# Linear attention with a feed-forward network: the first two query chunks loaded and prepared ahead of the values

## The chip, the cores and the metric

The kernel runs on one core of a Trainium2 chip. The time is that of the device for one launch, in microseconds (us). Engines are named as the profile does: PE is TensorE (its weight loads, which overlap, are PEld), DVE is VectorE, ACT is ScalarE, POOL is GpSimd, SP is SyncE. Loads and stores are DMA transfers that one of the engines issues.

## The reference

Eight batches of cosformer attention (8 heads, 576 rows, 64 columns each) are followed by a multiplicative feed-forward network (FFN) over all 4608 rows:

```python
def phi(x, c, s):
    r = np.maximum(x, 0.0)
    return np.concatenate([r * c, r * s], axis=-1)
q_p = phi(q, cos_w, sin_w)          # cos and sin of pi/2 * row / 576
k_p = phi(k, cos_w, sin_w)
kv = np.einsum('bhsf,bhsd->bhfd', k_p, v)
z = np.sum(k_p, axis=2)
num = np.einsum('bhsf,bhfd->bhsd', q_p, kv)
den = np.einsum('bhsf,bhf->bhs', q_p, z)[..., None] + 1e-06
x = (num / den)                      # heads side by side: 4608 x 512
out = (((x @ w1) * (x @ w2)) @ w3) @ w_out
```

The features of a row are 128 wide: 64 cosine and 64 sine values. No row of a batch can be finished before all keys and values of its batch have gone into the sums kv and z.

## The kernel before

**The work and its stages.** Each batch is cut into chunks of 128 rows (the fifth has 64), with all heads side by side. The chunks of batch 0 go through these steps, each with a name and line that the profile shows:

- Features of a chunk (`features`): VectorE makes the cosine half (L273), ScalarE the sine half (L277). With `scalar_heads=4`, ScalarE makes the sine half of four heads and VectorE that of the other four (L280). `prep_k` and `prep_q` call it for keys (kp) and queries (qp).
- `prep_v` copies a chunk of the values next to a column of ones (va, L300), so that one matmul gives kv and z together.
- `kv_first` runs the 40 key-value matmuls of batch 0 (5 chunks x 8 heads, L325) into two PSUM banks, four heads in each, kva and one half of a pnum tile, and copies them to kvs (L331).
- `q_tr` transposes the features of a query chunk with eight matmuls into a PSUM tile pst (L339); the copy to qpT is left to the caller by VectorE (first returned function) or ScalarE (second, L342). `q_tr_halves` does the same in two halves with a VectorE copy each (L352, L353).
- `num` makes the numerator and denominator of a chunk with eight matmuls (L368), and VectorE divides (L384 to L386) into xblk. With `chain=False` the division is returned, to be placed later.
- `x_tr` transposes xblk with four matmuls (L420) and copies the result into xT (L422), by VectorE or by ScalarE. xT is what the FFN multiplies (`products`, L465).

**The order.** The kernel is scheduled by hand: each engine carries out its instructions in the order in which the program gives them. First comes the setup, with the loads of batch 0. SyncE issues the keys in f32; GpSimd issues the rest with a conversion to bf16: values, the last 64 rows of the values, query chunks 0 and 1, chunks 2 and 3, then the FFN weights. Further loads (`other_loads`) are let go by a GpSimd copy that reads the first xblk. `idle_mms(n)` runs n matmuls on zeros whose result nobody reads, to keep TensorE busy while it has nothing to do.

Then comes the part in which the change lies, written out by hand: features of the keys, values, sums, features and transposes of the first query chunks, the first two numerators. After it the FFN begins, in 40 + 24 x 8 groups; between groups stand the steps of attention that the planner put into numbered slots. Slot 1, after the first 16 FFN matmuls, holds `x_tr` of chunk 1, the transposes of query chunk 3 and `num` of chunk 2; slot 3 and slot 5 hold the next ones:

```python
at(1, lambda: x_tr(0, 1, by_vector=True), lambda: q_tr(0, 3, evac=False)[1](), lambda: num(0, 2))
at(3, lambda: x_tr(0, 2), lambda: num(0, 3))
at(5, lambda: x_tr(0, 3))
```

PSUM tiles: ps_tr holds two pst tiles, used in turn by all transposes; ps_att holds one pnum tile, ps_first the numerator of chunk 0.

Of the kernel before, what the change touches and what calls it, by code (L numbers as in the profile page):

```python
# [68 lines left out]
def kernel(  # L69
# [11 lines left out]
    nc = tc.nc  # L81
# [49 lines left out]
    def load_first(eng, t, src, c0=0, n=4, b=0):  # L131
        rows = src[b, :, 0:512, :].rearrange("h (p j) d -> p h j d", j=4)
        eng.dma_start(out=t[:, :, c0:c0 + n, :].rearrange("p h j d -> p h (j d)"),  # L133
                      in_=rows[:, :, c0:c0 + n, :].rearrange("p h j d -> p h (j d)"))

    def load_first4(eng, t, src, b=0):
        eng.dma_start(out=t[0:64, :, 4, :], in_=src[b, :, 512:S, :].rearrange("h p d -> p h d"))
# [19 lines left out]
    v0 = raw[0, "v"] = ld.tile([P, H, NCH, D], BF16, name="vs")  # L157
    load_first(nc.sync, k0, k)
    load_first4(nc.sync, k0, k)
    load_first(nc.gpsimd, v0, v)  # L160
    zeros = const.tile([P, 512], BF16, name="zeros")
    nc.vector.memset(zeros[:], 0.0)
    va_bufs, kp_bufs, qp_bufs = [], [], []
# [19 lines left out]
    def idle_mms(n):  # L183

        for _ in range(n):
            nc.tensor.matmul(unread[:, :], lhsT=zeros[:, 0:128], rhs=zeros[:], start=True, stop=True)

    idle_mms(27)
    cosv, sinv = _trig_tables(nc, const)
    identb = const.tile([P, P], BF16, name="identb")  # L190
    load_first4(nc.gpsimd, v0, v)
    load_first(nc.gpsimd, q0, q, 0, 2)
    make_identity(nc, identb[:])
    load_first(nc.gpsimd, q0, q, 2, 2)
    def load_w12(c0, n):
# [58 lines left out]
    feat = {}  # L254

    def feat_of(b):
        if b not in feat:
            feat[b] = (kp_bufs[b % 2], qp_bufs[b % 2], va_bufs[b % 2])
        return feat[b]
# [8 lines left out]
    def features(b, dst, src, c, cos=True, sin=True, scalar_heads=H):  # L268

        R = ROWS[c]  # L270
        at = c if b in (0, B - 1) else NCH + c
        if cos:
            nc.vector.tensor_scalar(out=dst[:R, c, :, 0:D], in0=src[:R, :, c, :], scalar1=0.0,  # L273
                                    scalar2=cosv[:R, at:at + 1], op0=ALU.max, op1=ALU.mult)
        if sin:
            n = scalar_heads
            nc.scalar.activation(out=dst[:R, c, 0:n, D:F], in_=src[:R, 0:n, c, :], func=ACTF.Relu,  # L277
                                 scale=sinv[:R, at:at + 1], bias=0.0)
            if n < H:
                nc.vector.tensor_scalar(out=dst[:R, c, n:H, D:F], in0=src[:R, n:H, c, :],  # L280
                                        scalar1=0.0, scalar2=sinv[:R, at:at + 1],
                                        op0=ALU.max, op1=ALU.mult)
# [6 lines left out]
    def prep_k(b, c):  # L289
        features(b, feat_of(b)[0], raw[b, "k"], c)  # L290

    def prep_q(b, c):
        features(b, feat_of(b)[1], raw[b, "q"], c)
        if c in dma_q(b):
            transpose_q(b, c)
# [21 lines left out]
    def kv_first():  # L317

        kp, qp, va = feat[0]
        kvs = sm.tile([P, H, D + 1], BF16, name="kvs", bufs=2)  # L320
        kvb = ps_att.tile([P, 2, 512], FP32, name="pnum")
        halves = (kva[:, :], kvb[:, 0, :])
        for c in range(NCH):
            for h in range(H):
                nc.tensor.matmul(halves[h // 4][:, ds((h % 4) * 65, 65)], lhsT=kp[:, c, h, :],  # L325
                                 rhs=va[:, c, h, 0:D + 1], start=(c == 0 and h % 4 == 0),
                                 stop=(c == NCH - 1 and h % 4 == 3))
        att_of(0)["kvs"] = kvs
        yield
        for half in range(2):  # L330
            nc.scalar.copy(out=kvs[:, 4 * half:4 * half + 4, :], in_=halves[half][:, 0:260])  # L331
        yield

    def q_tr(b, c, evac=True):
        R = ROWS[c]
        qp = feat[b][1]
        pst = ps_tr.tile([P, 8, 128], BF16, name="pst")
        for h in range(H):
            nc.tensor.transpose(pst[:, h, :], qp[:, c, h, :], identb[:])  # L339
        dst, src = att_of(b)["qpT"][:, :, ds(columns_of(b, c), R)], pst[:, :, 0:R]  # L340
        on_vector = lambda: nc.vector.tensor_copy(out=dst, in_=src)
        on_scalar = lambda: nc.scalar.copy(out=dst, in_=src)  # L342
        if evac:
            on_vector()
        return on_vector, on_scalar

    def q_tr_halves(b, c):

        for half in range(2):
            pst = ps_tr.tile([P, 8, 128], BF16, name="pst")  # L350
            for i in range(4):
                nc.tensor.transpose(pst[:, i, :], feat[b][1][:, c, 4 * half + i, :], identb[:])  # L352
            nc.vector.tensor_copy(out=att_of(b)["qpT"][:, ts(half, 4), ds(columns_of(b, c), 128)],  # L353
                                  in_=pst[:, 0:4, :])

    def num(b, c, chain=True, in_two=False):
        rows = out_rows(b, c)
        R = ROWS[c]
        at = columns_of(b, c) - rows.start
        qpT, kvs = att[b]["qpT"], att[b]["kvs"]  # L360
        if b == 0 and c == 0:
            nt = ps_first.tile([P, 2, 512], FP32, name="pfirst")
        else:
            pool = more_att[0] if more_att and order_of(b).index(c) % 2 == 0 else ps_att
            nt = None if in_two else pool.tile([P, 2, 512], FP32, name="pnum")
        banks = [ffn_tile(), ffn_tile()] if in_two else [nt[:, g, :] for g in range(2)]
        for h in range(H):
            nc.tensor.matmul(banks[h // 4][:, ds((h % 4) * 65, 65)], lhsT=qpT[:, h, ds(at, 128)],  # L368
                             rhs=kvs[:, h, :], start=True, stop=True)
        if b < 2:  # L370
            rows, R = slice(0, P), P
        if in_two:
            parts = [(slice(g, g + 1), t[rows, 0:260].rearrange("p (g h e) -> p g h e", g=1, e=65))
                     for g, t in enumerate(banks)]
        else:
            parts = [(slice(0, 2), nt[rows, :, 0:260].rearrange("p g (h e) -> p g h e", e=65))]
        xblk = sm.tile([P, 2, 4, D], BF16, name="xblk", bufs=4)
        att[b]["x"][c] = xblk

        def normalize():  # L380
            den = sm.tile([P, 2, 4], FP32, name="den")
            for g, n4 in parts:
                G = g.stop - g.start
                nc.vector.tensor_scalar_add(out=den[rows, g], in0=n4[:, :, :, 64], scalar1=1e-6)  # L384
                nc.vector.reciprocal(out=den[rows, g], in_=den[rows, g])
                nc.vector.tensor_tensor(out=xblk[rows, g], in0=n4[:, :, :, 0:D],  # L386
                                        in1=den[rows, g].unsqueeze(3).to_broadcast([R, G, 4, D]),
                                        op=ALU.mult)

        if chain:  # L390
            normalize()
        return normalize
# [11 lines left out]
    def x_tr(b, c, by_vector=False):  # L404
        R, rows = ROWS[c], out_rows(b, c)
        xblk = att[b]["x"].pop(c)
        xf = xblk[:].rearrange("p g h d -> p (g h d)")
        if b % 2 == 0:
            slot = S * b + 128 * c
        else:  # L410
            slot = S * b + (0 if c == 4 else 64 + 128 * c)
        t, o = divmod(slot, 512)
        if t not in xT:
            xT[t] = xtp.tile([P, 4, 512], BF16, name="xT")
        if b >= 2 or (b, c) in ((0, 4), (1, 3)):
            nc.sync.dma_start_transpose(out=xT[t][:, :, ds(o, R)], in_=xf[rows])
            return
        pst = ps_tr.tile([P, 8, 128], BF16, name="pst")
        for kc in range(4):
            nc.tensor.transpose(pst[:, kc, :], xf[:, ts(kc, 128)], identb[:])  # L420
        copy = nc.vector.tensor_copy if by_vector else nc.scalar.copy
        copy(out=xT[t][:, :, ds(o, R)], in_=pst[:, 0:4, rows])  # L422
# [168 lines left out]

    for c in range(NCH):
        prep_k(0, c)
    for c in range(NCH):
        prep_v(0, c)
    kv_steps = kv_first()
    next(kv_steps)
    q0f = feat[0][1]
    features(0, q0f, q0, 0, scalar_heads=4)
    next(kv_steps)  # L600
    prep_q(0, 1)
    idle_mms(2)
    q_tr_halves(0, 0)
    prep_q(0, 2)
    idle_mms(1)
    num(0, 0)
    q_tr(0, 1, evac=False)[1]()
    other_loads(att[0]["x"][0][:, 0, 0, 0:1])
    features(0, q0f, q0, 3, sin=False)
    features(0, q0f, q0, 3, cos=False)  # L610
    idle_mms(2)
    x_tr(0, 0, by_vector=True)
    num(0, 1)
    q_tr(0, 2, evac=False)[1]()
    ps_ffn = []
    for stack in first:
        stack.close()
# [82 lines left out]
```

## Time and profile before

| what | value |
|---|---|
| time, median of 3 | 247.64 us (247.55 to 247.78) |
| span of the profiled execution | 245.9 us |
| PE busy | 238.0 us, 97% |
| DVE busy | 138.2 us, 56% |
| ACT busy | 130.3 us, 53% |
| POOL busy | 94.1 us, 38% |
| granted TensorE clock | 1.0 |
| first FFN matmul | 16.0 us after the start of the span |

The shares are over the whole span. Nearly all of it is the FFN, in which TensorE goes without a pause; the change touches only the first 18 us. There the timeline, the chain of waits and the time from issue to landing of each load are the views to read. Times in them are counted from the start of the span. A transfer's landing is its issue plus its time to landing.

### The profile page before, as it was taken

Reading aid. Unit: us, or ns where it says so; the run is one execution under the profiler, and the core shown is the slowest. Engines: PE = TensorE matmul, PEld = TensorE weight load, DVE = VectorE, ACT = ScalarE, POOL = GpSimd, SP = SyncE. Lnnn points to the kernel's source line nnn. Section 1 sums busy time; section 2 is a strip of 40 time slices with the busy share of each in tenths; the row PEclk is TensorE's granted clock in tenths of the full one; section 3 lists DMA queues with packets and bytes.
Section 4 is the critical chain, followed back from the end, with each engine's and each line's share of the span. In section 5 each row is a group of like instructions: output and inputs, shape, how many; then the busy total and the mean of one; then the engine's idle time right before and its main releaser. Section 6 shows DMA issues by size and latency. Waiting matters only on the chain.

```text
span 245.9 us, 5011 instructions
## 1 busy us (share of the span) xinstructions
PE 238.0 (97%) x1842; PEld 130.7 (53%) x1872; DVE 138.2 (56%) x344; ACT 130.3 (53%) x266; POOL 94.1 (38%) x196
## 2 busy tenths in 40 slices
PE   8799999999999999999999999999999999999994
PEld 3479555566965445455554545455545554444443
DVE  7775663668976655656674565657564544312420
ACT  2675324856943693576377546663674233434332
POOL 7655352124412162228032603451331005978700
PEclk9999999999999999999999999999999999999999
DMA  6999999999989979979999999999996227998923
GB/s 194 182 197 200 206 206 202 194 185 170 151 156 119 187 106 170 182 107 161 182 130 136 178 136 133 168 129 187 143 122 119 54 54 224 256 300 277 290 87 128
DMA packets 86200, 41.22 MB, mean 168 GB/s; under 512 B 53792, under 2 KB 82720, under 8 KB 86176
## 3 DMA queue, kind: packets, MB, share of 16 engines
q0 software_dynamic: 37008, 27.20, 71.4%
q1 hardware_dynamic: 49168, 13.71, 35.9%
q8 instruction: 14, 0.23, 0.4%
q14 instruction: 10, 0.08, 0.1%
HBM read 38.80 MB, written 9.44 MB: 196 GB/s over the span
## 4 chain that ended last, share of the span: by engine, by line
PE 92%; DMA 3%; issue 1%; DVE 1%; POOL 1%; ACT 0%; POOLq 0%
PE ffnps L465 50%; PE ffnps L535 24%; PE ffnps L240 6%; PE pnum L368 4%; PE pnum L308 4%; DMA qs<-in_q_dram 3%; PE pst L226 1%; PE pst L339 1%; PE pst L420 1%; PE ffnps L551 1%; POOL vs L133 0%; DVE xblk L386 0%; PE pfirst L368 0%; PE ffnps L368 0%; DVE qpT L353 0%
## 5 line engine op out<-in xcount | busy, mean ns | idle before, releaser
L465 PE MATMUL ffnps<-xT,w2b 128*128 128x512 bf16 (+2 forms) x337 | 75.0, 343 | 0.5
L465 PE MATMUL ffnps<-xT,w1b 128*128 128x512 bf16 (+2 forms) x335 | 74.5, 343 | 0.3
L522 DVE TENSOR_TENSOR abT<-asb,ffnps 128x512 bf16<-128x512 bf16 x64 | 43.9, 685 | 49.1 <-PE ffnps L465 44.8
L518 ACT CAST asb<-ffnps 128x512 bf16<-128x512 f32 x64 | 37.4, 585 | 52.5 <-PE ffnps L465 45.1
L535 PE MATMUL ffnps<-w34b,abT 128*128 128x512 bf16 x270 | 63.5, 379 | 0.5
L570 POOL COPY seen<-mark 1x1 bf16<-1x1 bf16 x50 | 9.0, 179 | 101.1 <-ACT mark L568 101.1
L465 PEld LDWEIGHTS <-w2b 128*128 128x128 bf16 x344 | 30.9, 98 | 26.8
L465 PEld LDWEIGHTS <-w1b 128*128 128x128 bf16 x344 | 30.9, 98 | 26.6
L535 PEld LDWEIGHTS <-abT 128*128 128x128 bf16 x280 | 26.0, 98 | 27.9
L542 ACT COPY osb<-ffnps 128x512 f32<-128x512 f32 x35 | 20.4, 584 | 31.4 <-PE ffnps L535 31.4
L277 ACT ACTIVATE qp<-qs,sinv 128x512 bf16<-128x512 bf16 (+2 forms) x40 | 28.1, 716 | 1.6 <-DMA qs<-in_q_dram 1.6
L277 ACT ACTIVATE kp<-ks,sinv 128x512 bf16<-128x512 bf16 (+1 forms) x35 | 24.8, 719 | 4.1 <-DMA ks<-in_k_dram 4.1
L386 DVE TENSOR_TENSOR xblk<-pnum,den 128x512 bf16<-128x512 f32 (+1 forms) x37 | 25.6, 691 | 1.3
L450 POOL DMA_DIRECT2D out_dram<-osb x42 | 22.1, 531 | 3.0 <-issue 2.1
L300 POOL COPY va<-vs 128x512 bf16<-128x512 bf16 (+1 forms) x30 | 17.8, 629 | 6.4 <-DMA vs<-in_v_dram 4.3
L368 PEld LDWEIGHTS <-qpT 128*128 128x128 bf16 x320 | 15.4, 98 | 8.7 <-DVE qpT L353 0.6
L384 DVE TENSOR_SCALAR den<-pnum 128x8 f32<-128x8 f32 (+1 forms) x37 | 6.1, 164 | 22.2 <-PE pnum L368 21.9
L273 DVE TENSOR_SCALAR qp<-qs,cosv 128x512 bf16<-128x512 bf16 (+1 forms) x40 | 16.7, 425 | 0.7 <-DMA qs<-in_q_dram 0.7
L368 PE MATMUL pnum<-kvs,qpT 128*128 128x65 bf16 x296 | 15.7, 194 | 0.1
L240 PE MATMUL ffnps<-woutb,w3T 128*128 128x512 bf16 x61 | 15.1, 379 | 0.2
L273 DVE TENSOR_SCALAR kp<-ks,cosv 128x512 bf16<-128x512 bf16 (+1 forms) x35 | 12.3, 370 | 2.5 <-DMA ks<-in_k_dram 2.5
L308 PEld LDWEIGHTS <-kp 128*128 128x128 bf16 x280 | 11.3, 98 | 3.8
(88 smaller groups left out, 182.5 us busy)
## 6 DMA issues: line engine op xcount, KB each, us to landing
out_dram<-osb POOLq DMA_DIRECT2D x16, 256.0 KB, 4.3
out_dram<-osb POOLq DMA_DIRECT2D x24, 128.0 KB, 3.8
qs<-in_q_dram POOLq DMA_DIRECT2D x8, 256.0 KB, 6.6
ks<-in_k_dram POOLq DMA_DIRECT2D x6, 320.0 KB, 6.0
qs<-in_q_dram POOLq DMA_DIRECT2D x6, 320.0 KB, 7.6
vs<-in_v_dram POOLq DMA_DIRECT2D x6, 320.0 KB, 6.0
ks<-in_k_dram POOLq DMA_DIRECT2D x6, 256.0 KB, 7.9
vs<-in_v_dram POOLq DMA_DIRECT2D x6, 256.0 KB, 6.4
```

Source lines behind the costliest of these rows:

```text
L240: nc.tensor.matmul(acc[:, :], lhsT=w3T[:, lc % 4, :], rhs=woutb[:, lc, :], start=(lc == 0), stop=(lc == 7))
L273: nc.vector.tensor_scalar(out=dst[:R, c, :, 0:D], in0=src[:R, :, c, :], scalar1=0.0, scalar2=cosv[:R, at:at + 1], op0=ALU.max, op1=ALU.mult)
L277: nc.scalar.activation(out=dst[:R, c, 0:n, D:F], in_=src[:R, 0:n, c, :], func=ACTF.Relu, scale=sinv[:R, at:at + 1], bias=0.0)
L308: nc.tensor.matmul(kvt[:, h // 4, ds((h % 4) * 65, 65)], lhsT=kp[:, c, h, :], rhs=va[:, c, h, 0:D + 1], start=(i == 0 and h % 4 == 0), sto ...
L368: nc.tensor.matmul(banks[h // 4][:, ds((h % 4) * 65, 65)], lhsT=qpT[:, h, ds(at, 128)], rhs=kvs[:, h, :], start=True, stop=True)
L386: nc.vector.tensor_tensor(out=xblk[rows, g], in0=n4[:, :, :, 0:D], in1=den[rows, g].unsqueeze(3).to_broadcast([R, G, 4, D]), op=ALU.mult)
L450: eng.dma_start(out=rows[:, :, cols], in_=osb[64 * i:64 * i + rows.shape[0], :, cols])
L465: nc.tensor.matmul(out, lhsT=w[:, kc, ts(jc, 128)], rhs=x[:, kc, tok], start=(kc == 0), stop=(kc == 3))
L518: nc.scalar.copy(out=asb[:], in_=aT[:, :])
L522: nc.vector.tensor_mul(out=abT[:, jc, :], in0=asb[:], in1=bT[:, :])
L535: nc.tensor.matmul(ops[:, :], lhsT=abT[:, jc, ts(ms, 128)], rhs=w34b[:, jc, :], start=(jc == 0), stop=(jc == 7))
L542: nc.scalar.copy(out=osb[:, ms % 2, :], in_=ops[:, :])
```

## The change

The loads of query chunks 0 and 1 are issued before those of the values. Their features, and the transposes of both chunks, stand ahead of the value copies and the key-value matmuls, so that they can be made while the values land. The key-value sums are copied out of PSUM by ScalarE and VectorE, half each, instead of by ScalarE alone. The features of chunk 2 and 3, the copies of the transposes and the division of chunk 1 take other places in the queues; `x_tr` of chunk 0 is copied by ScalarE instead of VectorE, and the number of idle matmuls changes from 2, 1 and 2 to 7, 1 and 1.

```diff
-    load_first(nc.gpsimd, v0, v)
+    load_first(nc.gpsimd, q0, q, 0, 2)
...
+    load_first(nc.gpsimd, v0, v)
     load_first4(nc.gpsimd, v0, v)
-    load_first(nc.gpsimd, q0, q, 0, 2)
     make_identity(nc, identb[:])
     load_first(nc.gpsimd, q0, q, 2, 2)
...
-        for half in range(2):
-            nc.scalar.copy(out=kvs[:, 4 * half:4 * half + 4, :], in_=halves[half][:, 0:260])
+        for half, copy in enumerate((nc.scalar.copy, nc.vector.tensor_copy)):
+            copy(out=kvs[:, 4 * half:4 * half + 4, :], in_=halves[half][:, 0:260])
...
     for c in range(NCH):
         prep_k(0, c)
+    feat_of(0)
+    q0f = feat[0][1]
+    features(0, q0f, q0, 0, scalar_heads=4)
+    prep_q(0, 1)
+    idle_mms(7)
+    q_tr(0, 0, evac=False)[1]()
+    second = q_tr(0, 1, evac=False)[1]
     for c in range(NCH):
         prep_v(0, c)
     kv_steps = kv_first()
     next(kv_steps)
-    q0f = feat[0][1]
-    features(0, q0f, q0, 0, scalar_heads=4)
     next(kv_steps)
-    prep_q(0, 1)
-    idle_mms(2)
-    q_tr_halves(0, 0)
-    prep_q(0, 2)
+    second()
     idle_mms(1)
     num(0, 0)
-    q_tr(0, 1, evac=False)[1]()
+    prep_q(0, 2)
     other_loads(att[0]["x"][0][:, 0, 0, 0:1])
-    features(0, q0f, q0, 3, sin=False)
-    features(0, q0f, q0, 3, cos=False)
-    idle_mms(2)
-    x_tr(0, 0, by_vector=True)
-    num(0, 1)
+    idle_mms(1)
+    divide = num(0, 1, chain=False)
+    x_tr(0, 0)
+    divide()
     q_tr(0, 2, evac=False)[1]()
+    features(0, q0f, q0, 3)
```

## The prediction

> **What bounds the kernel now.** I read the page first: the shares by engine, then the chain that ended last. TensorE is busy for 97% of the span and carries the chain nearly alone:
>
> ```profile
> PE 92%; DMA 3%; issue 1%; DVE 1%; POOL 1%; ACT 0%; POOLq 0%
> ```
>
> The 3% of DMA is one wait of 8 us at the start. So I asked for the chain in order of time (start us, length us, what), where the change lies:
>
> ```profile
> 3.56 8.04 DMA qs<-in_q_dram
> ...
> 11.63 0.35 DVE qp L273
> ...
> 12.20 0.41 PE pst L352 x4
> ...
> 13.11 0.30 PE pfirst L368 x4
> ...
> 13.78 0.18 DVE den L384
> ...
> 14.22 0.70 DVE xblk L386
> ...
> 14.97 0.40 PE pst L420 x4
> 15.37 0.36 PE pnum L368 x8
> 15.73 0.45 PE pst L339 x8
> 16.18 0.89 PE ffnps L465 x16
> ```
>
> The reader is to see two things. The start is bound by the landing of the first two query chunks at 11.6 us; from there one chain runs through features, transposes, numerator, division and transpose to the first FFN matmul (its group starts at 16.01 us in the timeline). And from 16 us on the chain is TensorE alone. The waits of TensorE and of its weight loads, asked for from 16 us to the end, hold one row in all:
>
> ```profile
> PEld L339 <- ACT qp L277: 0.4, 1, 0.4
> ```
>
> So there is no slack later that could swallow a delay or lose a gain: the end moves by what TensorE's queue gains or loses before about 18 us. Next I read when the loads land, from the tiles' answers (values, then queries):
>
> ```profile
> DMA to landing us min/median/max: 7.5/8.0/8.4
> DMA to landing us min/median/max: 8.0/8.0/11.9
> ```
>
> Values of rows 0 to 511 are issued at 1.28 and land at 9.7; their last 64 rows, issued at 2.87, land at 10.4; query chunks 0 and 1, issued at 3.56, land at 11.6; chunks 2 and 3, issued at 5.03, at 13.0. Last the timeline (start, us, what), for durations and for the queue of ScalarE:
>
> ```profile
> 9.87 1.09 DVE L300 COPY va<-vs 128x512 bf16<-128x512 bf16 x5
> 12.05 0.35 ACT L331 CAST kvs<-kva 128x260 bf16<-128x260 f32 x1
> 12.57 1.34 ACT L277 ACTIVATE qp<-qs,sinv 128x512 bf16<-128x512 bf16 x2
> 14.23 1.01 ACT L342 COPY qpT<-pst 128x1024 bf16<-128x1024 bf16 x1 [0.32 <-PE pst L339]
> 17.27 0.61 PE L339 MATMUL pst<-identb,qp 128*128 128x128 bf16 x8
> ```
>
> The value copies begin when VectorE is done with the key features, just after the landing; a transposed chunk costs ScalarE 1.01, a sine half 0.72 (0.62 from start to start, two in 1.34); and the transpose of query chunk 3 starts at 17.27.
>
> [...] the first key-value copy, whose sums ended at about 11.7, waits behind a sine half and starts at 12.05. [...] here the values, issued at 1.28, land 2.9 us after the keys' 6.84. [...] In this trace 1.3 us idle before 10.20 cost no clock; the gaps that I find below are under 0.7 us, so I cost them no clock.
>
> **The change part by part.**
>
> *Loads reordered.* The same three transfers stand in the ring before 11.6, the pair of query chunks now first. The pair took 11.6-10.4 = 1.2 us behind the values, the last 64 rows 0.66. So the pair should land at 9.7-1.2 = 8.5, the values at 11.61-0.66 = 10.95 and their last rows at 11.6. The landing of query chunks 2 and 3 (13.0) and of the weights behind them doesn't move.
>
> *Features and transposes of chunks 0 and 1 moved ahead.* ScalarE is busy with the key sines till then: five from 6.91, a start each 0.61, free at 9.99. Its queue: half-width sine of chunk 0, 9.99 to 10.50; sine of chunk 1, 10.40 to 11.12. VectorE is free at 9.86; its cosines (0.35) and half sine (0.28) end by 10.7, before the values. TensorE: 27 idle matmuls to 8.9, seven more at 0.21 to 10.2, hidden in waiting. Transposes of chunk 0 at 10.55, of chunk 1 at 11.12+0.05 = 11.17, eight at 0.056, free at 11.61. ScalarE copies chunk 0 out from 11.20 to 12.21. This takes 1.5 us of work (11.61 to 13.11) off the query path, but it is queued ahead of the key-value matmuls.
>
> *Key-value sums.* First value copy 10.95 to 11.25, its matmuls could start at 11.3, but stand behind the second transpose: 11.61. They start 0.031 apart, 40 of them: the last at 12.86 (10.20 to 11.44 before). So the sums come 1.42 us later than before.
>
> *Copies on two engines.* ScalarE's half 12.97 to 13.33; VectorE's half (0.43, L314) 13.09 to 13.52. One engine would need 0.26 longer start to start, so this saves about 0.1. The numerator's first four heads go at 13.38, the last four at 13.57, last start 13.68, denominator 0.23 later at 13.91 (before 13.78: **+0.13**). Moving the query work ahead thus exchanges a chain that ends at 13.78 for one that ends at 13.91.
>
> *Division and its transpose.* Same operations: product at 14.35 to 15.04, transpose 15.09 (numerator 1 now stands before it, in a wait). The copy to xT goes from VectorE (0.42) to ScalarE (0.59): 15.51 to 16.10, FFN starts at **16.15** against 16.01. Transposes of chunk 2 need a cosine that stands behind the product on VectorE (14.95 to 15.30) and go at 15.35, free at 15.8: hidden.
>
> *Features of chunk 3 moved behind.* ScalarE's queue after its key-value half, in order: the copy of chunk 1, 13.23 to 14.24; sine 2, to 14.9; the xT copy, 15.51 to 16.10 as above; the copy of chunk 2, 16.00 to 17.01; sine 3, 16.92 to 17.63. In the kernel before, sine 3 ran at 15.14. The transposes of chunk 3 wait for it: **17.68** instead of 17.27. Ahead of them on TensorE are 16 FFN matmuls and four transposes, done at 17.3 (16.15+0.94+0.22). So TensorE stands about 0.37 us, and behind that wait in its queue are numerator 2 and all the FFN. From there, as before, 0.70 to the next FFN matmul: 18.39 instead of 17.98, **+0.41**.
>
> *Rest.* The later loads are let go by the first product, 0.13 later[...]. Fewer idle matmuls at 14 us and one division fewer in a slot change no sum. End: 247.64+0.41 = 248.05.
>
> **The rivals.**
>
> *Forecast: ScalarE's order costs what the earlier queries gain* (0.60). +0.41, with some 0.15 of handoffs to either side, so it lies just within 0.2% (0.50 us), or just over.
>
> *The values become the bound* (0.28). The margin is small: TensorE is free for the sums at 11.61, which a landing up to 11.28 meets, and I work out 10.95. [...] Landing between 11.6 and 12.1 delays all by 0.3 to 0.8: 248.4 to 248.9. For it: nothing in this trace shows the loads in this order. Against it: the sum of the three transfers is measured, and only the short last rows follow the values.
>
> *The hiding pays* (0.12). If the sums went with the landing of the values at 11.3 instead of behind the transposes (0.3 gained), and if the keys landed some 0.3 earlier [...] (0.3 more, as their sines hold ScalarE till 9.99), the FFN would start 0.6 before my 16.15, at 15.55; with the wait for sine 3 gone as well only that start counts: 247.64-0.46 = 247.2, and with a tenth more 247.1, which is faster. For it: the query path of 1.5 us does leave the chain, and ScalarE has a gap of 0.6 between 14.9 and 15.5. Against it: the order on TensorE puts the sums behind the transposes, sine 3 stands behind the xT copy in an engine that goes in order, and nothing in the change touches the keys' own load.
>
> **How the numbers follow.** The likeliest case gives 248.05. Of its 0.60, 0.42 lies within 0.2% and 0.18 beyond it. Of the late values' 0.28, 0.25 is slower and 0.03 within. Of the last 0.12, 0.09 is faster and 0.03 within. Sums: faster 0.09, same 0.48, slower 0.43. The range goes from 247.3, which leaves out most of the hiding that pays, to 248.9, the upper end of the late values: what is left out is about 0.15.
>
> **What would show it right or wrong.** Value copies starting at about 11.0 (over 11.3: the second case); key-value matmuls at 11.6, directly behind the second transpose; denominator at 13.9; first FFN matmul at 16.15, released by ScalarE; a new wait of TensorE on ScalarE's sine before the transposes at 17.7; FFN again at 18.4. If the transposes of chunk 3 don't wait, the ScalarE step is wrong; if TensorE shows new waits after 20 us or a lower clock, the claim that only the start moves is.

## The result, and the profile after

The changed kernel takes 248.57 us (median of 22 executions, 248.11 to 248.99), the kernel before 247.70 beside it (22 executions): a ratio of 1.0032, 95% interval 1.0023 to 1.0041. It is slower by 0.87 us where 0.41 was forecast. Measured twice more, the difference was 0.64 and 0.69.

The chain that ended last no longer contains a wait for a load. First its shares on the page, then the chain in order of time (start us, length us, what):

```profile
PE 97%; ACT 1%; DVE 1%; issue 0%
```

```profile
1.19 10.26 PE unread L186 x34
11.45 0.89 PE pst L339 x16
12.34 0.13 PE kva L325 x4
...
13.52 0.38 ACT kvs L331
...
13.95 0.49 PE pfirst L368 x8
...
14.46 0.18 DVE den L384
...
14.90 0.70 DVE xblk L386
...
16.08 0.58 ACT xT L422
16.67 0.99 ACT qpT L342
17.65 0.63 ACT qp L277
...
18.33 0.62 PE pst L339 x8
18.95 0.26 PE pnum L368 x8
19.21 1.77 PE ffnps L465 x24
```

The eight microseconds of waiting for the queries are gone from it. In their place stand two things: 34 idle matmuls that end at 11.45, directly followed by the query transposes, and three ScalarE steps in a row, the copy to xT, the copy of chunk 2 and the sine half of chunk 3, which end in the transposes of chunk 3. The 24 FFN matmuls that follow the numerator of chunk 2 stand at 19.21 in this chain, at 18.14 in that of the kernel before: 1.07 later, and the span is 1.0 longer. Of the 1.07, 0.71 is there at the first FFN matmul (16.72 against 16.01); the other 0.36 comes after it.

Two answers on waits carry this. First the waits of weight loads on ScalarE's sine halves, from 16 us to the end (us in total, times, longest):

```profile
PEld L339 <- ACT qp L277: 0.9, 2, 0.5
```

The kernel before has one such wait, of 0.4, after 30 us, and the changed kernel has it too. The new one is at 18.33, as the timeline shows, where idle time and its releaser stand in brackets; the first FFN matmul stands above it:

```profile
16.72 0.38 PE L465 MATMUL ffnps<-xT,w1b 128*128 128x128 bf16 x4
...
18.33 0.45 PEld L339 LDWEIGHTS <-qp 128*128 128x128 bf16 x8 [0.51 <-ACT qp L277]
18.33 0.62 PE L339 MATMUL pst<-identb,qp 128*128 128x128 bf16 x8 [0.34 <-ACT qp L277]
```

Then the weight loads of the idle matmuls in the first 13 us, of the kernel before and of the changed kernel:

```profile
PEld L186 <- issue: 2.2, 8, 0.3
```

```profile
PEld L186 <- issue: 3.6, 13, 0.3
```

A gap of 0.28 us appears before each weight load while an idle matmul takes 0.43 us; after that they follow each other at 0.21. So the idle matmuls start at half rate; the granted clock reads 1.00 there, and why they start so was not shown (last section). In the profile of the kernel before, eight ran at half rate, in that of the changed kernel thirteen. Five more of these, 0.21 us each, are 1.1 us. In the kernel before nobody waited for them: 27 idle matmuls ended at 8.9 and the next matmul had its values at 10.2. In the changed kernel seven more stand between them and the query transposes.

### The profile page after: what moved, and what is told of

Its sections match the earlier page's. It is cut to its first block, busy times and chain, and to the rows that moved or that the text cites. A ratio compares the mean times of both kernels' runs of the same rounds, so it can differ in the third digit from the quotient of the medians.

```text
span 246.9 us, 5050 instructions
## 1 busy us (share of the span) xinstructions
PE 241.4 (98%) x1876; PEld 131.6 (53%) x1876; DVE 138.4 (56%) x342; ACT 131.8 (53%) x267; POOL 93.5 (38%) x196
## 3 DMA queue, kind: packets, MB, share of 16 engines
q1 hardware_dynamic: 49168, 13.71, 36.1%
## 4 chain that ended last, share of the span: by engine, by line
PE 97%; ACT 1%; DVE 1%; issue 0%
PE ffnps L465 50%; PE ffnps L535 24%; PE ffnps L240 6%; PE unread L186 4%; PE pnum L368 4%; PE pnum L308 4%; PE pst L226 1%; PE pst L339 1%; PE ffnps L551 1%; PE pst L420 1%; ACT qpT L342 0%; DVE xblk L386 0%; PE kva L325 0%; ACT qp L277 0%; ACT xT L422 0%; PE ffnps L368 0%
## 5 line engine op out<-in xcount | busy, mean ns | idle before, releaser
L465 PE MATMUL ffnps<-xT,w1b 128*128 128x512 bf16 (+2 forms) x344 | 75.5, 344 | 0.1
L535 PE MATMUL ffnps<-w34b,abT 128*128 128x512 bf16 x280 | 65.2, 379 | 0.0
L273 DVE TENSOR_SCALAR qp<-qs,cosv 128x512 bf16<-128x512 bf16 (+1 forms) x40 | 17.2, 438 | 0.0
```

What stands on the lines that cost most here:

```text
L465: nc.tensor.matmul(out, lhsT=w[:, kc, ts(jc, 128)], rhs=x[:, kc, tok], start=(kc == 0), stop=(kc == 3))
L535: nc.tensor.matmul(ops[:, :], lhsT=abT[:, jc, ts(ms, 128)], rhs=w34b[:, jc, :], start=(jc == 0), stop=(jc == 7))
```

## The experiments

**The idle matmuls or ScalarE's order.** Four variants of the changed kernel on one chip, beside the kernel before at 247.64. The first is without the seven idle matmuls:

```diff
     prep_q(0, 1)
-    idle_mms(7)
     q_tr(0, 0, evac=False)[1]()
```

> The changed kernel without the seven idle matmuls ahead of the first query transposes. Theory (the idle matmuls stand in the way: in the changed kernel's trace 13 of the first 34 ran at 0.43 us each and they ended at 11.45, when the features had been ready since about 10.9): transposes at 10.4, sums at 11.4 instead of 12.18, some 0.6 us faster than the changed kernel, so about 248.0, with a narrower spread of its runs. Rival 1 (ScalarE's order alone makes the loss): no change, 248.6. Rival 2 (the idle matmuls keep the clock up): slower transposes and sums, 249 or more.

Measured: 248.13 (15 executions), ratio to before 1.0025, interval 1.0014 to 1.0035; single ones up to 249.63. Its trace has 14 idle matmuls at half rate, one more than the changed kernel's, and yet the transposes start at 10.43, as soon as the features are there. So the seven did stand in the way in the changed kernel's first profile. By the medians, leaving them out takes 0.15 to 0.4 off the loss of 0.64 to 0.87. The fastest execution gains nothing: 0.71 above the fastest of the kernel before, 0.74 in the first measurement of the changed kernel. The spread did not narrow, which the theory had wrong. With fourteen:

```diff
-    idle_mms(7)
+    idle_mms(14)
```

> The changed kernel with 14 idle matmuls instead of seven ahead of the first query transposes. Theory (idle matmuls on the path): seven more at 0.213 us, 1.5 us in all, slower by nearly all of that: 249.9 to 250.1. Rival 1 (hidden in a wait for the features): less than 0.5 us slower, under 249.1.

Measured: 250.11 (4 executions), ratio 1.0096, interval 1.0079 to 1.0113. That is 1.5 us over 248.57 and 1.8 over the changed kernel's next measurement: all of the 1.5 us of seven more lies on the path. In its profile the 41 end at 12.34 and the transposes follow at once. Next the sine half of chunk 3 goes ahead of the copy to xT:

```diff
     prep_q(0, 2)
+    features(0, q0f, q0, 3, cos=False)
     other_loads(att[0]["x"][0][:, 0, 0, 0:1])
...
-    features(0, q0f, q0, 3)
+    features(0, q0f, q0, 3, sin=False)
```

> The changed kernel with the sine half of query chunk 3 on ScalarE directly behind that of chunk 2, in the gap before the copy to xT. Theory (ScalarE's order holds the transposes of chunk 3 by 0.5 us): no wait of TensorE on that sine any more, FFN again 0.4 to 0.5 us earlier, 248.1. Rival 1 (idle matmuls make all of the loss): no change, 248.6. Rival 3 (the sine only moves the wait to the copy of xT or of chunk 2): 248.4 to 248.7.

Measured: 247.76 (21 executions), ratio to before 1.0005, interval 0.9998 to 1.0012. The end of its chain:

```profile
15.55 0.59 ACT xT L422
16.15 0.04 issue
16.19 1.05 PE ffnps L465 x16
17.25 0.22 PE pst L420 x4
17.47 0.45 PE pst L339 x8
17.91 0.26 PE pnum L368 x8
18.18 1.77 PE ffnps L465 x24
```

From the first FFN matmul on the chain is TensorE alone; the two ScalarE steps between xT and the transposes of chunk 3 have left it. The gain of 0.8 was more than the wait of 0.5. Both edits together, no idle matmuls and the sine moved:

> The changed kernel without the seven idle matmuls and with the sine of chunk 3 behind that of chunk 2. If both causes act in series, the gains add: 0.6 and 0.45 off 248.57, about 247.5 to 247.7, level with the kernel before. If one hides behind the other: not under 248.0.

Measured: 247.81 (14 executions), from 247.22 to 250.37, ratio 1.0014, interval 0.9997 to 1.0032. That is just above the 247.5 to 247.7 expected of gains that add, and in the median no faster than the sine moved alone (247.76). The profiled execution was one of the two long ones, 249.78. Its stretches (us, length, PE busy and instructions, PEld, DVE, ACT, POOL, granted clock, DMA, GB/s):

```profile
9.00:10.00 1.00, 0.00 (x0) 0.00 (x0) 1.00 (x3) 1.00 (x3) 0.74 (x1) 1.00 1.46 199
10.00:11.00 1.00, 0.00 (x0) 0.00 (x0) 0.87 (x4) 1.00 (x3) 0.00 (x0) 1.00 1.84 175
11.00:12.00 1.00, 0.97 (x11) 0.97 (x12) 0.56 (x3) 0.58 (x1) 0.00 (x0) 0.59 1.85 180
12.00:13.00 1.00, 1.00 (x15) 1.00 (x14) 0.53 (x3) 1.00 (x1) 0.00 (x0) 0.50 1.61 191
13.00:14.00 1.00, 1.00 (x22) 1.00 (x20) 0.00 (x0) 0.01 (x1) 0.00 (x0) 0.50 1.44 195
14.00:15.00 1.00, 0.89 (x19) 0.82 (x18) 0.07 (x1) 0.20 (x1) 0.00 (x0) 0.71 1.46 199
```

Here eight idle matmuls ran at half rate, so the 27 ended early, at 8.7; and the keys landed late (their features start at 7.34, at 6.64 in the changed kernel's first profile), so that the query features were ready only at 11.0. TensorE stood for 2.3 us, and the clock granted to it read 0.59, 0.50, 0.50 and 0.71 in the four microseconds from 11.00 on, just when the transposes and the sums ran. In its chain 16 transposes take 1.79 us (0.89 in the changed kernel) and four sums 0.22 (0.13). Against the version with three idle matmuls (below), the transposes start 0.7 later, and transposes and sums take 1.3 longer. So in these profiles idle matmuls that quicken late cost time with the seven; ones that quicken early, together with late keys, cost time without them. How often either happens was not measured.

**Where the rest of the gain came from.** The changed kernel was run again beside others:

> The changed kernel itself once more, beside the others of this call, as the measure for them. Theory [...]: again 248.2 to 249.0, the profile's FFN late by as much as its idle matmuls end after about 10.5. Rival (the difference of the first measurement was its chip's): under 248.2.

Measured: 248.32 (12 executions, 248.00 to 249.85), ratio 1.0029, interval 1.0013 to 1.0045. The profiled execution had 14 idle matmuls at half rate and took 249.07. And again, on a third chip, with the version with the sine moved next to it:

> The changed kernel beside the next one on the same chip. 248.2 to 248.7.

> The changed kernel with the sine half of chunk 3 behind that of chunk 2, again, now beside the changed kernel. Theory (the wait for the sine is the 0.5 us that the trace shows[...]): 0.4 to 0.5 us under the changed kernel of this call. Rival (the earlier sine brings more than its wait): 0.7 us or more under it.

Measured: 248.44 (21 executions; ratio 1.0027, interval 1.0019 to 1.0036) and 248.03 (13 executions; ratio 0.9997, interval 0.9985 to 1.0010), 0.41 between the medians, as the theory had it; but the ratios, each to the executions of the kernel before, are 0.3% apart, some 0.7 us, which was the rival's figure. So the times alone don't settle the size. The traces do: from the first FFN matmul to the 24 that follow numerator 2 it takes 2.49, 2.49 and 2.50 in the three profiles of the changed kernel, 1.98 or 1.99 in the five with the sine moved and TensorE's order unchanged (some are below), and 2.13 in the kernel before. What the first 0.8 held besides is not shown. The profile of this run of the changed kernel, which took 248.09, is worth a look, as its kernel is the same, line by line:

```profile
PEld L186 <- issue: 2.2, 8, 0.3
```

```profile
10.39 1.23 PE pst L339 x16
...
13.74 0.18 DVE den L384
...
15.36 0.59 ACT xT L422
15.94 0.99 ACT qpT L342
16.93 0.63 ACT qp L277
...
17.61 0.62 PE pst L339 x8
18.23 0.26 PE pnum L368 x8
18.49 1.77 PE ffnps L465 x24
```

With eight idle matmuls at half rate the 34 end at 10.33, before the features are there. All that follows comes 0.7 us earlier than in the first profile, and the wait for the sine of chunk 3 remains.

**The parts of the change alone.** The new order of loads in the kernel before, with nothing else moved:

```diff
-    load_first(nc.gpsimd, v0, v)
+    load_first(nc.gpsimd, q0, q, 0, 2)
...
+    load_first(nc.gpsimd, v0, v)
     load_first4(nc.gpsimd, v0, v)
-    load_first(nc.gpsimd, q0, q, 0, 2)
```

> The kernel before with the new order of the loads alone; features, transposes and copies stand where they were. Theory (the loads swap who waits, their sum is the same): values land at 11.0, sums start at 11.3 and end at 12.6, the features of the queries stand behind the value copies on VectorE, the first numerator comes at about 13.9: 248.3 to 248.7. Rival (the landing of the queries is all that bounds the start): faster than before, under 247.3.

Measured: 248.82 (7 executions, up to 251.37), ratio 1.0062, interval 1.0034 to 1.0090. Values landed at 11.2 and the first denominator came at 14.87, later than expected: on TensorE the transposes of chunk 0 stand behind the sums, which now end later, and two idle matmuls, so that the first numerator starts at 14.21 instead of 13.11. The opposite, the changed kernel with the loads in the old order (the same diff reversed):

> The changed kernel with the loads in the old order, values ahead of query chunks 0 and 1. Theory (the sums stand behind the query transposes on TensorE, whatever has landed): queries at 11.6, transposes of chunk 0 at 12.2 and of chunk 1 at 12.8, sums from 13.3, 1.2 to 2 us slower than the changed kernel: 249.6 to 250.4. Rival (the order of the loads doesn't matter): 248.3 to 248.6.

Measured: 249.88 (4 executions), ratio 1.0080, interval 1.0066 to 1.0094, 1.4 above the changed kernel beside it. The transposes start at 12.09 and the sums stand behind them. Each half of the change needs the other; together they come out near where the kernel was.

**Towards a better version.** Three idle matmuls and the sine moved:

```diff
-    idle_mms(7)
+    idle_mms(3)
```

> The changed kernel with three idle matmuls instead of seven and the sine half of chunk 3 behind that of chunk 2. Theory (idle matmuls cost time where they end late and hold the clock where they end early): at or a little under the version with seven and the sine moved (247.76), 247.5 to 247.7, with few or no runs over 249. Rival (three are too few to hold the clock): single runs at 249.5 and more, as without idle matmuls.

Measured: 247.59 (14 executions, 247.42 to 248.25), ratio 0.9996, interval 0.9988 to 1.0004. Level with before, and no execution over 248.25; fourteen executions can't rule out rare long ones. Then the second transposes behind the sums, and xT by VectorE:

```diff
-    second = q_tr(0, 1, evac=False)[1]
     for c in range(NCH):
         prep_v(0, c)
     kv_steps = kv_first()
     next(kv_steps)
+    second = q_tr(0, 1, evac=False)[1]
...
-    x_tr(0, 0)
+    x_tr(0, 0, by_vector=True)
```

> As the version with three idle matmuls and the sine moved, and the transposes of chunk 1 behind the key-value sums, and the copy of chunk 0 to xT by VectorE. Theory (the start is then bound by the landing of the values): sums at about 11.35, first denominator at 13.65 (13.78 in the kernel before), FFN at 15.8 (16.01): 247.3 to 247.5, faster than before by 0.1%. Rival (the wait comes back elsewhere, on the copy of chunk 1 before the second numerator): 247.7 to 248.0.

Measured: 247.80 (14 executions), ratio 1.0006, interval 0.9997 to 1.0014: no gain, in the range of the rival. The values landed at 11.22 and the sums started at 11.60; the transposes of chunk 1, now behind them, held the numerator till 13.53, and the first denominator came at 13.98 where 13.65 was expected. Last, the version with three idle matmuls, with ScalarE making both key-value copies:

```diff
-    for half, copy in enumerate((nc.scalar.copy, nc.vector.tensor_copy)):
+    for half, copy in enumerate((nc.scalar.copy, nc.scalar.copy)):
```

> The version with three idle matmuls and the sine moved (247.59), but both halves of the key-value sums copied by ScalarE. Theory (ScalarE's second copy would start 0.26 after its first and end about where that of VectorE does, 0.1 later): 247.6 to 247.8. Rival (two engines halve a wait on the path): 0.3 slower or more, 247.9 and up.

Measured: 248.12 (22 executions), ratio 1.0017, interval 1.0007 to 1.0027, 0.5 above the version with two engines, which is the rival's range; but that one was measured on another chip. From the first copy to the denominator its trace takes 1.03 us (12.88 to 13.91), against 0.93 (12.78 to 13.71) with two engines: the 0.1 of the theory. The copy to xT then waits for ScalarE, so that the FFN starts 3.32 after the first copy instead of 3.19. The rest may be the idle matmuls, which ended late in its profile (10.8, 14 at half rate); this comparison doesn't settle what the second engine is worth.

**One number for all of them.** For each profiled execution, the start of the 24 FFN matmuls in the chain, and the device time less that start (all in us):

| kernel | FFN at | time | difference |
|---|---|---|---|
| before | 18.14 | 247.65 | 229.5 |
| changed, first profile | 19.21 | 248.70 | 229.5 |
| changed, again | 19.31 | 249.07 | 229.8 |
| changed, third | 18.49 | 248.09 | 229.6 |
| no idle matmuls | 18.61 | 248.34 | 229.7 |
| 14 idle matmuls | 20.10 | 249.57 | 229.5 |
| sine moved | 18.18 | 248.05 | 229.9 |
| no idle matmuls, sine moved | 19.97 | 249.78 | 229.8 |
| three idle matmuls, sine moved | 17.96 | 247.42 | 229.5 |
| loads alone | 19.23 | 248.82 | 229.6 |
| changed, old loads | 20.19 | 249.80 | 229.6 |
| sine moved, again | 18.60 | 248.16 | 229.6 |
| both key-value copies by ScalarE | 18.19 | 247.74 | 229.6 |
| transposes of chunk 1 behind the sums | 18.34 | 248.40 | 230.1 |

What happens before that start is what the time shows, to within 0.6 us. The two largest differences, 230.1 and 229.9, belong to profiles with a later wait of a weight load on VectorE's abT, of 0.9 and 0.7 us. The second profile with the sine moved has no such wait.

## Why the prediction was right in its way and short in size

The range held the time and the direction was right, but the outcome that it gave most weight, within 0.2%, was missed: 0.32%, and 0.27 to 0.29% in the repeats. The forecast's mechanism, ScalarE's order, is there at the forecast size; a second one, the idle matmuls, was put at nothing.

- *Only the start counts.* Right: the table above.
- *Loads.* Right: query chunks forecast to land at 8.5, values at 10.95, last rows at 11.6. In the first profile the query features start at 9.8, straight behind the key features, without a wait for the load, and the value copies, which wait for the landing, at 11.03. The rival of late values did not come: TensorE came to the sums at 12.2, a microsecond after.
- *Idle matmuls.* This step failed: "seven more at 0.21 to 10.2, hidden in waiting". It took the length of the slow phase from one profile (and 8.9 plus seven at 0.21 is 10.4, not 10.2, still before the transposes that it put at 10.55). With eight at half rate 34 end at 10.33, with thirteen at 11.45, and the profiles here have between 8 and 14. In the first profile of the changed kernel this made the first denominator 14.46 instead of 13.91 and the FFN 16.72 instead of 16.15. In the third profile, where it did hold, the steps came at 13.74 (13.91 forecast), 15.99 (16.15), 17.61 for the transposes of chunk 3 (17.68) and 248.09 for the time (248.05). That the total agrees so well is in part luck: this was the second fastest of 21 executions, whose median is 248.44.
- *Copies on two engines.* The traces agree in size: 0.1 from the first copy to the denominator. The times of that comparison leave it open.
- *ScalarE's order.* Right: TensorE waits for the sine of chunk 3, the matmul 0.34 us (0.37 forecast) and its weight load 0.51. Against the kernel before, the stretch from the first FFN matmul on is 0.36 longer (2.49 to 2.13). Moving the sine took 0.41 off the median beside the changed kernel.
- *The hiding pays.* It did not in this form: in its best execution the changed kernel took 248.00. That the clock could fall in a gap was put at no cost, for gaps under 0.7 us. None of the profiles of the changed kernel shows a fall at the start (four sums take about 0.13 us in all three, and in the first the granted clock reads 1.00 in every microsecond to 18); without the seven and with the sine moved, in the profile above, a gap of 2.3 us was followed by one, to 0.50.

So the profiles show two parts: ScalarE's order and the later sums, 0.35 us in the third profile (FFN at 18.49 against 18.14), and from none to about 1 us more from idle matmuls that end late. The medians, 0.64 to 0.87 above before, would leave a share of 0.2 to 0.5 for the second. That share is only the remainder; how often they quicken late was not measured, since each run leaves one profile.

One thing doesn't fit. In all three measurements the fastest execution of the changed kernel lies 0.72 to 0.74 above the fastest of the kernel before (248.00 against 247.27, for example), though 0.4 would be expected of executions whose idle matmuls end early. The kernel before has executions there that are 0.3 to 0.4 faster than its one profiled one, and none of these was profiled; what makes them faster stays open.

## What to carry to other kernels

Work that hides a wait takes a place in a queue that goes in order, as ScalarE's did here (in the changed kernel's first chain, copy to xT at 16.08, copy of chunk 2 at 16.67, sine of chunk 3 at 17.65): ask of every piece that is moved ahead what now stands behind it, and of every piece moved back who waits for it. Here moving one ScalarE instruction by two places was worth about as much as all of the forecast loss (0.41 us between the medians on the third chip). Filler on an engine is harmless only while its end has slack in every execution; if its own speed varies, take the slowest that the profiles show, not the one at hand. In the kernel before it had that slack: the 27 ended at 8.9 in its profile, and with 14 at half rate, as in the profile of the loads alone, they end at 10.2, when its next matmul starts.

## What the runs showed of the hardware

The idle matmuls, 512 columns wide, take 0.43 us each at first and then 0.21, and the change comes at a time that differs between executions of the same program: after 13, 14 and 8 of them in the three profiles of the changed kernel. What sets that time was not shown. Where the granted clock reads 0.59 and then 0.50 (above), 16 transposes take twice their time, 1.79 us against 0.89. But at the start it reads 1.00. In the changed kernel (stretch, length, PE busy and instructions, granted clock, DMA, GB/s):

```profile
2.00:4.00 2.00, 2.00 (x6) 1.00 0.86 248
8.00:10.00 2.00, 2.00 (x11) 1.00 1.46 199
```

So the view of the clock doesn't show why the first ones are slow.

In one profile, that of no idle matmuls with the sine moved, the clock fell around a gap of 2.3 us: it read 0.59 in the microsecond in which work came back and 0.50 in the two after. Around a gap of 1.3 us in the kernel before, from 8.9 to 10.2, it read 1.00. How long a gap may be before the clock falls was not shown.
